# A fused transformer block: block 0's last attention sums travel by GpSimd's queue, and GpSimd starts splitting weights sooner

## The chip, the cores and the metric

The kernel runs on one core of one Trainium2 chip. The metric is device time in microseconds (us). Before the change the median of 3 runs was 1417.01 us (1413.06 to 1418.36).

## The reference

2048 rows of 512 features pass an attention layer with 32 query heads of 16 features that share one key and one value head, and then a gated feed-forward layer of width 1792. All is float32.

```python
h  = x + A(layernorm(x))          # A: q = x@wq (32 heads), k = x@wk, v = x@wv (one head)
                                  #    p = softmax(q k^T / 4); o = p v; A = o @ wo
h2 = h + B(layernorm(h))          # B: (gelu(x@w_gate) * (x@w_up)) @ w_down
```

## The kernel before

**Tiling.** The rows are cut into 4 blocks of 512 queries (`NB`), the heads into 8 groups of 4 (`NG`), the keys into 16 chunks of 128 (`KC`). For each block, group and chunk there are two `score` calls (L1031), numbered by `n`. One call makes 2 x 2 score matmuls `s<-qg,kaug` (L414) and one exponential `p<-s` on ScalarE (L418). After the second call of a chunk, four matmuls `acc<-p,v_sb` (L422) add the weighted values, some calls later (`finish`, L1008). A group takes 32 calls, block 0 takes 256. The query tile `qg` of a group is loaded from the DRAM buffer `q_d` one group ahead.

**The end of a group.** `evacuate` (L433) copies the finished PSUM sums to `oT` on VectorE (L435). They have to change partitions: SyncE stores `oT` to the DRAM buffer `acc_d` (L439), and `turn_out` (L444) reads it back in four transfers of 64 KB into `oc` (L448). For every second group VectorE then takes the reciprocal of the softmax sums in four pieces (L462), multiplies (L465), and splits the result into a high and a low part, `o_hi` (L473) and `o_lo` (L477). Four such columns c = 0 to 3 make up a block. For block 0 the store and the read of all groups but the last are spread over later calls. For its last group, `g == 7`, both are written straight behind the copy.

**The dense part.** A block's dense part begins with the output projection `pp<-wo,o` (L613, called from `project`, L660). It needs all four columns of `o_hi` and `o_lo`, in the order c = 0 to 3, and the split weights `wo`, which SyncE loads in two transfers of 1 MB (L587). For block 0, `load_wo(0)` stands in the program at `n == 256` (L1093), behind the last use of the pool "early", whose memory its tiles take over. The first `pp` matmul stands 16 calls later. Further on SyncE loads rows of x for the residual (`xb`, L647) and the first four gate and up weights (`w<-w_d`, L573, 512 KB each).

**Splitting the weights.** While block 0's attention runs, GpSimd prepares 46 pieces of weight (`part_weights`, L514): 4 of `wo`, and 14 each of gate, up and down. A raw piece of 256 KB is loaded on SyncE's queue (`load_f`, L520, issued at L522), two pieces ahead, into one of four buffers. GpSimd copies its high part and subtracts for its low part (L121, L122, called from `part_f`, L525), and stores both, 512 KB, one part later from one of two buffers (L531 and L537). The loop over `n` calls `next(parts)` at fixed counts (L1120): before the change at 16, 26 and 30 in the first group of 32, then seven times in each group.

**Bounds.** For each block of queries a bound `m` on the scores is worked out on GpSimd (L273 to L290) and stored to `q_d` (L294), two loop steps after its input is ready (`age`, L325). The tile of block 3's bound is in the pool "early", so `load_wo(0)` waits for this store too.

**What sets the order.** The engines run their own instruction streams, each in the written order. PE, ScalarE and GpSimd are scheduled by hand throughout, SyncE and VectorE in the loop over `n`. SyncE issues its transfers to one queue, GpSimd to another. An instruction waits for semaphores, and whatever stands behind it on its engine waits with it.

Of the kernel before, what the change touches and what calls it, by code (L numbers as in the profile page):

```python
# [32 lines left out]
AHEAD_W = 2  # L33
# [7 lines left out]
HURRY = ((0, 3), (1, 0), (1, 1))  # L41

START = 8

MIXED = {0: ("mms", 2), 3: ("smm", 1), 6: ("mm", 1), 8: ("ss", 1)}

# [8 lines left out]
def kernel(  # L55
# [12 lines left out]
    nc = tc.nc  # L68
# [3 lines left out]
    DH = wk.shape[1]  # L72
# [8 lines left out]
    NG = H // 4  # L81
    KC = S // P
# [28 lines left out]
    acc_d = dram.tile([P, 4, T], F32, name="acc_d")  # L111
# [5 lines left out]
    def split(eng_hi, hi, lo, src, eng_lo=None):  # L117
        if eng_hi is nc.scalar:
            nc.scalar.activation(hi, src, AF.Copy)
        else:  # L120
            eng_hi.tensor_copy(hi, src)  # L121
        (eng_lo or nc.vector).tensor_tensor(lo, src, hi.bitcast(F32), op=ALU.subtract)  # L122
# [29 lines left out]
    def attend(first):  # L152
        with ExitStack() as outer:
            with tc.manual_schedule(
                engines={mybir.EngineType.PE, mybir.EngineType.Pool, mybir.EngineType.Activation}
            ):
                run(outer, first)


    def run(outer, first):  # L160
# [164 lines left out]
        def age():  # L325
            for entry in after:
                entry[0] -= 1
            while after and after[0][0] <= 0:
                after.pop(0)[1]()
# [99 lines left out]
        def take_out():  # L429
            for step in outs.pop(0):  # L430
                step()

        def evacuate(b, g, acc):  # L433
            oT = sb.tile([P, T], F32, tag="oT", bufs=2, name=f"oT_{b}_{g}")
            nc.vector.tensor_copy(oT, acc)  # L435
            c, k = divmod(g, 2)
            last = b == NB - 1 and g == NG - 1
            if not last:
                nc.sync.dma_start(acc_d[:, g % 4, :], oT)  # L439
            if k == 0:  # L440
                pair[0] = sb.tile([P, 2, T], F32, tag="oc", bufs=2, name=f"oc_{b}_{c}")
            oc = pair[0]

            def turn_out():  # L444
                view = acc_d[:, g % 4, :].rearrange("(j s e) t -> j e s t", s=2, e=DH)
                for j in range(4):
                    r0 = 64 * k + DH * j
                    nc.sync.dma_start(oc[r0 : r0 + DH, :, :], view[j])  # L448

            def gather():  # L450

                for s in (1, 0):
                    for j in range(4):
                        r0 = 64 * k + DH * j
                        (nc.sync if s or j == 0 else nc.scalar).dma_start(
                            oc[r0 : r0 + DH, s, :], oT[(2 * j + s) * DH : (2 * j + s + 1) * DH, :]
                        )


            def invert(t):  # L460
                sl = slice(t * P, (t + 1) * P)
                nc.vector.reciprocal(oc[:, 1, sl], oc[:, 1, sl])  # L462

            def divide():
                nc.vector.tensor_tensor(oc[:, 0, :], oc[:, 0, :], oc[:, 1, :], op=ALU.mult)  # L465

            def high():
                if c == 0:
                    o_blk[b] = [
                        sb.tile([P, DC, T], F32R, tag=f"o_{w}", bufs=1, name=f"o_{w}_{b}")  # L470
                        for w in ("hi", "lo")
                    ]
                nc.vector.tensor_copy(o_blk[b][0][:, c, :], oc[:, 0, :])  # L473

            def low():
                hi, lo = o_blk[b]
                nc.vector.tensor_tensor(  # L477
                    lo[:, c, :], oc[:, 0, :], hi[:, c, :].bitcast(F32), op=ALU.subtract
                )


            def piece(t):
                sl = slice(t * P, (t + 1) * P)
                hi, lo = o_blk[b]
                invert(t)
                nc.vector.tensor_tensor(
                    oc[:, 0, sl], oc[:, 0, sl], oc[:, 1, sl], op=ALU.mult
                )
                split(nc.vector, hi[:, c, sl], lo[:, c, sl], oc[:, 0, sl], nc.gpsimd)

            if b == 0 and g < NG - 1:
                outs.append([turn_out])
            elif not last:
                turn_out()
            if last:
                last_out.extend([piece, gather])
            elif k == 1:

                if b == 0:
                    outs.extend([[] for _ in range(11)])  # L500
                    outs.extend([partial(invert, t)] for t in range(TB))
                    outs.extend([step] for step in (divide, high, low))
                else:
                    outs.append([])
                    outs.extend([partial(invert, t), partial(invert, t + 1)] for t in (0, 2))
                    outs.append([divide, high, low])
            if b == 0 and g == NG - 1:
                while outs:
                    take_out()
# [4 lines left out]
        def part_weights(pw):  # L514

            def load_f(src, name):  # L520
                raw = pw.tile([P, D], F32, tag="w_raw", bufs=AHEAD_W + 2, name=f"{name}r")
                nc.sync.dma_start(raw.rearrange("p (c n) -> p c n", n=src.shape[-1]), src)  # L522
                return raw

            def part_f(name, raw):  # L525
                both = pw.tile([P, 2, D], F32R, tag="w_both", bufs=2, name=f"{name}b")
                split(nc.gpsimd, both[:, 0], both[:, 1], raw, nc.gpsimd)
                return both

            def store_1(f, k, both):  # L530
                nc.gpsimd.dma_start(  # L531
                    w1_d[2 * f + k].bitcast(F32),
                    both.rearrange("p i (c n) -> p i c n", c=DC).bitcast(F32),
                )

            def store_2(dst, both):
                nc.gpsimd.dma_start(dst.bitcast(F32), both.bitcast(F32))  # L537

            steps = [
                (  # L540
                    partial(load_f, wo_t[:, c : c + 1, :], f"wo{c}"),
                    partial(part_f, f"wo{c}"), partial(store_2, wo_d[c]),
                )
                for c in range(DC)
            ]
            for f in range(FC):
                fs = slice(f * P, (f + 1) * P)
                for k, src in enumerate((wg_t, wu_t)):
                    name = f"w1{f}_{k}"
                    steps.append((  # L550
                        partial(load_f, src[:, :, fs], name),
                        partial(part_f, name), partial(store_1, f, k),
                    ))
                name = f"w2{f}"
                steps.append((
                    partial(load_f, wd_t[:, f : f + 1, :], name),
                    partial(part_f, name), partial(store_2, w2_d[f]),
                ))
            raws, left = {i: steps[i][0]() for i in range(AHEAD_W)}, None
            for i, (_, part, store) in enumerate(steps):  # L560
                if left is not None:
                    left()
                if i + AHEAD_W < len(steps):
                    raws[i + AHEAD_W] = steps[i + AHEAD_W][0]()
                both = part(raws.pop(i))
                left = partial(store, both)
                yield 1
            left()
# [491 lines left out]
        n, lead = 0, 2 * PER + sum(SIZES[: LEAD[0]])  # L1060
        with tc.manual_schedule(engines={mybir.EngineType.SP, mybir.EngineType.DVE}):
            parts = None
            if first:
                work = later_q()
                parts = part_weights(early.enter_context(tc.tile_pool(name="parts", bufs=1)))

            token, left = None, 6 * (NB - 1) * DC * DC
            while n < lead:
                age()
                r = n % (2 * KC) if n >= 2 * KC else n - START if n < 28 else 30  # L1070
                if first and n == START:
                    token = next(work)
                if (token is None or token == REST and left <= 0) and (n < START or n % 2 == 0):
                    kinds, runs = "ss", 1
# [7 lines left out]
                if n == 2 * PER:  # L1082
# [7 lines left out]
                    parts = work = None  # L1090
# [25 lines left out]
                for _ in range(runs):  # L1116
                    if outs and not pause[0] and n % (2 * KC) not in (2, 3, 4):
                        take_out()
                    pause[0] = max(pause[0] - 1, 0)
                if parts is not None and n > 12 and n % (2 * KC) % 10 in (0, 6):  # L1120
                    next(parts, None)
            assert n == lead
        assert not outs
# [21 lines left out]
        for c in range(LEAD[0], (NB - 1) * NG * len(SIZES)):  # L1145
            b, cb = divmod(c, NG * len(SIZES))
# [400 lines left out]
```

## Time and profile before

| | us |
|---|---|
| median of 3 runs | 1417.01 |
| lowest, highest | 1413.06, 1418.36 |
| the profiled execution, own time | 1414.98 |
| its span, first to last instruction | 1413.2 |
| its mean granted TensorE clock | 0.997 |

The profiled execution lies 2.03 us below the median, and 1.78 us of its time are outside the span. All times of events below count from the start of the span. In the rows of a timeline the columns are start, duration, engine, line, operation, output<-input with the form, count, and in brackets the idle time ahead of it with what ended it. "SPq" rows are SyncE's issues of transfers: the time is that of issuing, not of moving. In the chain of waits a row is start, length and what the chain passes through. In the table of windows each engine's busy time stands with its instructions in brackets, then PEclk, the granted TensorE clock as a share of full speed, the busy share of the DMA engines, and GB/s.

### The profile page before, as it was taken

Reading aid. Unit: us, or ns where it says so; the run is one execution under the profiler, and the core shown is the slowest. Engines: PE = TensorE matmul, PEld = TensorE weight load, DVE = VectorE, ACT = ScalarE, POOL = GpSimd, SP = SyncE. Lnnn points to the kernel's source line nnn. Section 1 sums busy time; section 2 is a strip of 40 time slices with the busy share of each in tenths; the row PEclk is TensorE's granted clock in tenths of the full one; section 3 lists DMA queues with packets and bytes.
Section 4 is the critical chain, followed back from the end, with each engine's and each line's share of the span. In section 5 each row is a group of like instructions: output and inputs, shape, how many; then the busy total and the mean of one; then the engine's idle time right before and its main releaser. Section 6 shows DMA issues by size and latency. Waiting matters only on the chain.

```text
span 1413.2 us, 25646 instructions
## 1 busy us (share of the span) xinstructions
PE 1393.7 (99%) x10646; PEld 784.9 (56%) x10646; DVE 548.3 (39%) x982; ACT 1041.6 (74%) x1149; POOL 188.7 (13%) x286
## 2 busy tenths in 40 slices
PE   8999999999999999999999999999999999999998
PEld 7433333334555555555555555554565555557886
DVE  7322322324252433424252432513353342427665
ACT  7799999996777777777787777877788777772000
POOL 6455655521000000000000000000000000002000
PEclk9999999999999999999999999999999999999999
DMA  4477787762342332223252332223243241335551
GB/s 159 148 222 250 247 252 248 227 216 90 102 157 64 117 117 87 87 84 142 83 176 72 116 117 87 87 90 118 102 139 108 87 146 50 137 122 198 186 196 60
DMA packets 84969, 194.11 MB, mean 137 GB/s; under 512 B 9904, under 2 KB 24240, under 8 KB 84812
## 3 DMA queue, kind: packets, MB, share of 16 engines
q1 hardware_dynamic: 77572, 167.50, 35.4%
q0 software_dynamic: 7104, 24.78, 4.8%
q8 instruction: 86, 1.41, 0.4%
q14 instruction: 39, 0.32, 0.1%
q10 hardware_dynamic: 168, 0.10, 0.0%
HBM read 142.52 MB, written 49.55 MB: 136 GB/s over the span
## 4 chain that ended last, share of the span: by engine, by line
PE 92%; ACT 3%; DMA 2%; DVE 1%; issue 1%; POOL 0%; SPq 0%; DVEq 0%; ACTq 0%; POOLq 0%
PE acc L422 33%; PE s L414 18%; PE pu L936 9%; PE pg L936 8%; PE pd L936 4%; PE pq L412 4%; PE pd L613 3%; ACT p L418 3%; PE pd L635 3%; PE pg L635 3%; PE pu L635 3%; PE pp L613 2%; PE pp L744 1%; DMA acc_d<-oT 1%; PE pxt L680 1%
## 5 line engine op out<-in xcount | busy, mean ns | idle before, releaser
L418 ACT ACTIVATE p<-s 128x1024 f32<-128x1024 f32 x1024 | 970.2, 1032 | 229.0 <-PE s L414 226.0
L422 PE MATMUL acc<-p,v_sb 128*32 128x512 f32 x4096 | 496.9, 600 | 0.0
L414 PE MATMUL s<-qg,kaug 50*128 50x512 f32 x1984 | 418.1, 425 | 3.5 <-ACT p L418 3.5
L414 PEld LDWEIGHTS s<-qg,kaug 50*128 50x128 f32 x1984 | 195.1, 185 | 218.5 <-ACT p L418 121.5
L422 PEld LDWEIGHTS acc<-p,v_sb 128*32 128x32 f32 x4096 | 109.8, 109 | 229.0 <-issue 225.5
L936 PE MATMUL pu<-x2h,w 64*128 64x512 f32 x672 | 212.1, 391 | 0.0
L936 PE MATMUL pg<-x2h,w 64*128 64x512 f32 x672 | 211.7, 391 | 0.0
L936 PEld LDWEIGHTS pu<-x2h,w 64*128 64x128 f32 x672 | 116.0, 186 | 14.5
L936 PEld LDWEIGHTS pg<-x2h,w 64*128 64x128 f32 x672 | 116.3, 186 | 13.1 <-DVE h L878 0.5
L936 PE MATMUL pg<-x2l,w 64*128 64x512 f32 x336 | 122.3, 391 | 0.0
L936 PE MATMUL pu<-x2l,w 64*128 64x512 f32 x336 | 121.9, 390 | 0.0
L813 ACT ACTIVATE ga<-ga 128x512 f32<-128x512 f32 x56 | 35.3, 634 | 89.2 <-DVE ga L808 89.2
L131 POOL TENSOR_SCALAR rstd<-mv 128x1 f32<-128x1 f32 x16 | 3.5, 220 | 682.9 <-DVE mv L129 682.8
L936 PE MATMUL pd<-w,gh 64*128 64x512 f32 x384 | 81.2, 392 | 0.0
L878 DVE TENSOR_TENSOR h<-h,pd 128x512 f32<-128x512 f32 x48 | 31.9, 685 | 115.4 <-PE pd L936 66.4
L462 DVE RECIPROCAL oc<-oc 128x128 f32<-128x128 f32 x64 | 56.6, 923 | 32.4 <-DMA oc<-acc_d 27.6
L1172 DVE SCALAR_TENSOR_TENSOR ga<-ga,g 128x512 f32<-128x512 f32 x70 | 48.3, 691 | 52.3 <-ACT ga L813 51.3
L797 DVE COPY g<-pg 128x512 f32<-128x512 f32 x56 | 38.7, 692 | 63.0 <-PE pg L936 57.3
L936 PEld LDWEIGHTS pu<-x2l,w 64*128 64x128 f32 x336 | 58.0, 186 | 6.8
L936 PEld LDWEIGHTS pg<-x2l,w 64*128 64x128 f32 x336 | 58.2, 186 | 6.4
L435 DVE COPY oT<-acc 128x512 f32<-128x512 f32 x32 | 22.1, 692 | 96.8 <-PE acc L422 96.6
L810 DVE SCALAR_TENSOR_TENSOR g<-g,pu 128x512 f32<-128x512 f32 x56 | 38.2, 683 | 40.4 <-PE pu L936 30.5
(246 smaller groups left out, 1458.0 us busy)
## 6 DMA issues: line engine op xcount, KB each, us to landing
w<-w_d SPq DMA_DIRECT2D x112, 512.0 KB
w<-w_d SPq DMA_DIRECT2D x28, 1024.0 KB
qg<-q_d SPq DMA_DIRECT2D x48, 200.0 KB
q_d<-qh SPq DMA_DIRECT2D x32, 256.0 KB
wo<-wo_d SPq DMA_DIRECT2D x8, 1024.0 KB
acc_d<-oT SPq DMA_DIRECT2D x31, 256.0 KB
oc<-acc_d SPq DMA_DIRECT2D x124, 64.0 KB
w_d<-w_0b POOLq DMA_DIRECT2D x14, 512.0 KB, 7.3
```

The lines of the kernel that those rows point to most:

```text
L412: step()
L414: nc.tensor.matmul(s[:, a, :], kaug[rows, kc * P : (kc + 1) * P], qg[rows, 2 * u + a, :], start=True, stop=True,)
L418: nc.scalar.activation(p[:, 2 * u : 2 * u + 2, :], s, AF.Exp, scale=SCALE)
L422: nc.tensor.matmul(acc[32 * j : 32 * j + 32, :], v_sb[:, kc, :], p[:, j, :], start=(kc == 0), stop=(kc == KC - 1), skip_group_check=True,)
L462: nc.vector.reciprocal(oc[:, 1, sl], oc[:, 1, sl])
L613: nc.tensor.matmul(banks[k], lhsT[rows], rhs[rows], start=(turn == 0 and i == 0), stop=(turn == 1 and i == n - 1), skip_group_check=True,)
L635: nc.tensor.matmul(bank, lhsT, rhs, start=(i == 0), stop=(i == len(ts) - 1))
L797: nc.vector.tensor_copy(g, pg)
L810: nc.vector.scalar_tensor_tensor(g, g, 0.5, pu, op0=ALU.mult, op1=ALU.mult)
L813: nc.scalar.activation(a, a, AF.Tanh, scale=GELU_A * GELU_C)
L936: nc.tensor.matmul(e["bank"], lhsT[rows], rhs[rows], start=i == 0 and not e["both"], stop=last and e["both"], skip_group_check=True,)
L1172: (soon or lazy).pop(0)()
```

## The change

It has three parts.

1. For block 0's last group alone, the store of `oT` to `acc_d` and the four reads into `oc` are issued by GpSimd and no longer by SyncE.
2. The first two raw pieces, of `wo`, are loaded by GpSimd and no longer by SyncE.
3. `next(parts)` is called at n = 8, 11, 16, 21, 26 and 30 in the first group (it was 16, 26 and 30). All later parts stand three calls of `next` earlier.

```diff
+EARLY_PARTS = (8, 11, 16, 21, 26)
...
             last = b == NB - 1 and g == NG - 1
+            queue = nc.gpsimd if b == 0 and g == NG - 1 else nc.sync
             if not last:
-                nc.sync.dma_start(acc_d[:, g % 4, :], oT)
+                queue.dma_start(acc_d[:, g % 4, :], oT)
...
-                    nc.sync.dma_start(oc[r0 : r0 + DH, :, :], view[j])
+                    queue.dma_start(oc[r0 : r0 + DH, :, :], view[j])
...
-            def load_f(src, name):
+            def load_f(src, name, queue=nc.sync):
                 raw = pw.tile([P, D], F32, tag="w_raw", bufs=AHEAD_W + 2, name=f"{name}r")
-                nc.sync.dma_start(raw.rearrange("p (c n) -> p c n", n=src.shape[-1]), src)
+                queue.dma_start(raw.rearrange("p (c n) -> p c n", n=src.shape[-1]), src)
...
-            raws, left = {i: steps[i][0]() for i in range(AHEAD_W)}, None
+            raws, left = {i: steps[i][0](queue=nc.gpsimd) for i in range(AHEAD_W)}, None
...
-                if parts is not None and n > 12 and n % (2 * KC) % 10 in (0, 6):
+                if parts is not None and (
+                    n in EARLY_PARTS or n > 2 * KC - 4 and n % (2 * KC) % 10 in (0, 6)
+                ):
                     next(parts, None)
```

Line numbers after the change are higher by 2 to 5.

The first place is the end of block 0 on SyncE. Its stream before, from the bound check `b_d` to block 0's first dense weights; `qg` and `xb` belong to block 1's second group and block 0's dense part:

```order
L1469 DMA b_d<-q2m 32x1
L587 DMA wo_0_3388<-wo_d 128x2x1024
L587 DMA wo_1_3390<-wo_d 128x2x1024
L439 DMA acc_d<-oT_7_3419 128x512
L448 DMA oc_3_3128<-acc_d 16x2x512 x4
L394 DMA qg_1_3433<-q_d 50x2x512 x2
L647 DMA xb_0_3458<-in_A_x_dram 128x512
L647 DMA xb_1_3460<-in_A_x_dram 128x512
```

The same stretch of SyncE's stream after the change:

```order
L1474 DMA b_d<-q2m 32x1
L590 DMA wo_0_3388<-wo_d 128x2x1024
L590 DMA wo_1_3390<-wo_d 128x2x1024
L396 DMA qg_1_3433<-q_d 50x2x512 x2
L650 DMA xb_0_3458<-in_A_x_dram 128x512
L650 DMA xb_1_3460<-in_A_x_dram 128x512
```

The store and the four reads have left it, and `qg`, `xb` and what follows no longer stand behind them. On GpSimd at that place, before, behind the last weight piece `w213` and block 3's bound `m`, the dense part's `rstd` came next:

```order
L537 DMA w_d<-w213b 128x1024
L273 TENSOR_SCALAR mm_0_3298<-q_70,k2m 32x1
L276 TENSOR_TENSOR mm_0_3298<-mm_0_3298,power 32x1
L279 TENSOR_SCALAR mm_0_3298<-mm_0_3298 32x1
L282 TENSOR_SCALAR mm_0_3298<-mm_0_3298,k2m 32x1
L290 TENSOR_SCALAR m_0_3299<-qn_0_3295,mm_0_3298 32x512
L294 DMA q_d<-m_0_3299 32x512
L131 TENSOR_SCALAR rstd_0_0_3662<-mv_0_0_3659 128x1
```

After the change:

```order
L540 DMA w_d<-w213b 128x1024
L275 TENSOR_SCALAR mm_0_3298<-q_70,k2m 32x1
L278 TENSOR_TENSOR mm_0_3298<-mm_0_3298,power 32x1
L281 TENSOR_SCALAR mm_0_3298<-mm_0_3298 32x1
L284 TENSOR_SCALAR mm_0_3298<-mm_0_3298,k2m 32x1
L292 TENSOR_SCALAR m_0_3299<-qn_0_3295,mm_0_3298 32x512
L296 DMA q_d<-m_0_3299 32x512
L442 DMA acc_d<-oT_7_3419 128x512
L451 DMA oc_3_3129<-acc_d 16x2x512 x4
L133 TENSOR_SCALAR rstd_0_0_3662<-mv_0_0_3659 128x1
```

The five transfers stand between the bound and `rstd`. The second place is the start of the weight pieces on GpSimd; `kaug` is the last work for the keys. Before:

```order
L1359 TENSOR_TENSOR kaug<-vT_685,kaug 16x512 x2
L1359 TENSOR_TENSOR kaug<-vT_688,kaug 16x512 x2
L121 CAST wo0b<-wo0r 128x512
L122 TENSOR_TENSOR wo0b<-wo0r,wo0b 128x512
L537 DMA wo_d<-wo0b 128x1024
```

After:

```order
L1364 TENSOR_TENSOR kaug<-vT_685,kaug 16x512 x2
L1364 TENSOR_TENSOR kaug<-vT_688,kaug 16x512 x2
L525 DMA wo0r<-in_A_wo_dram 128x512
L525 DMA wo1r<-in_A_wo_dram 128x512
L123 CAST wo0b<-wo0r 128x512
L124 TENSOR_TENSOR wo0b<-wo0r,wo0b 128x512
L540 DMA wo_d<-wo0b 128x1024
```

GpSimd issues the first two raw loads itself, ahead of the first split. The streams of PE, ScalarE and VectorE hold the same instructions in the same order before and after.

## The prediction

> **What bounds the kernel now.** I read the page first: its busy times and the chain of work that ended last.
>
> ```profile
> PE 1393.7 (99%) x10646; PEld 784.9 (56%) x10646; DVE 548.3 (39%) x982; ACT 1041.6 (74%) x1149; POOL 188.7 (13%) x286
> PE 92%; ACT 3%; DMA 2%; DVE 1%; issue 1%; POOL 0%; SPq 0%; DVEq 0%; ACTq 0%; POOLq 0%
> ```
>
> PE is the bound nearly everywhere, so the change can earn only where PE stands still. The 2% of DMA in the chain deserve a look. In the chain in order of time they lie at the end of block 0:
>
> ```profile
> 299.21 1.17 ACT p L418
> ...
> 300.42 0.38 SPq L587
> 300.85 0.46 SPq L587
> ...
> 301.37 8.47 DMA acc_d<-oT
> ...
> 311.16 2.17 DMA oc<-acc_d
> ...
> 313.52 3.40 DVE oc L462 x4
> 316.95 0.70 DVE oc L465
> 317.67 0.44 DVE o_hi L473
> ...
> 318.16 1.02 PE pp L613 x4
> ```
>
> The store of 256 KB needs 8.47 us. Ahead of it on SyncE's queue stand the two `wo` loads (L587, 2 MB). The table of windows shows what the DMA engines did, and the timeline of PE what the wait costs:
>
> ```profile
> 298.00:300.00 2.00, 2.00 (x16) 0.53 (x12) 0.00 (x0) 2.00 (x3) 0.00 (x0) 1.00 0.00 0
> 302.00:304.00 2.00, 2.00 (x14) 0.60 (x14) 0.00 (x0) 2.00 (x4) 0.00 (x0) 1.00 0.92 365
> 318.29:321.70 3.41, 3.41 (x18) 1.56 (x22) 0.69 (x2) 1.94 (x2) 0.00 (x0) 0.52 1.03 414
> 311.42 0.49 PE L414 MATMUL s<-qg,kaug 50*128 50x512 f32 x2 [0.34 <-ACT p L418]
> 313.19 0.73 PE L613 MATMUL pp<-wo,o_hi 64*128 64x512 f32 x4 [0.34 <-DMA oc<-acc_d]
> 315.59 0.42 PE L414 MATMUL s<-qg,kaug 50*128 50x512 f32 x2
> 318.16 1.02 PE L613 MATMUL pp<-wo,o_hi 64*128 64x512 f32 x4 [2.14 <-DVE o_hi L473]
> ```
>
> At 365 GB/s the 2 MB alone last 5.7 us. PE starts `pp` at 313.19 with columns c = 0 to 2, and stands still for 2.14 us until 318.16, when column 3 of `o_hi` is there. Then comes a second loss: from 318.29 to 321.70 the granted clock is 0.52, with PE busy throughout, which costs (1 - 0.52) x 3.41 = 1.64 us. So the stall is worth at most 2.14 + 1.64 = 3.8 us, with the short wait at 313.19 4.1 us. Until 312 ScalarE's exponentials set PE's pace (its short waits are for `p`), and after 324 PE has work again, so a shorter stall moves all that follows.
>
> The Trainium skill, "TensorE: Matmul & The Clock Gate" (Part 1), says that the clock falls to half after a window of about 3.4 us with too little work, and that these windows run freely, not tied to the kernel. The row's 0.52 over 3.41 us agrees; by the page the 1.64 us would be paid in some executions only, and the sum would lie between -1.9 and -3.5.
>
> **The change, part by part.**
>
> *The store and the four reads on GpSimd.* What GpSimd's queue takes, and when the inputs are ready:
>
> ```profile
> 295.54 0.59 POOL L294 DMA_DIRECT2D q_d<-m  x1 [0.29 <-DMA oc<-acc_d]
> 331.07 0.24 POOL L131 TENSOR_SCALAR rstd<-mv 128x1 f32<-128x1 f32 x1 [34.94 <-DVE mv L129]
> 300.14 0.69 DVE L435 COPY oT<-acc 128x512 f32<-128x512 f32 x1 [11.34 <-PE acc L422]
> 49.77 1.04 POOL L348 DMA_DIRECT2D qg_first<-q_d  x2
> wo_d<-wo0b POOLq DMA_DIRECT2D x1, 512.0 KB, 2.9
> w_d<-w_0b POOLq DMA_DIRECT2D x14, 512.0 KB, 7.3
> w_d<-w211b POOLq DMA_DIRECT2D x1, 512.0 KB, 8.7
> q_d<-m POOLq DMA_DIRECT2D x3, 64.0 KB, 4.6
> qg_first<-m POOLq DMA_DIRECT2D x4, 2.0 KB, 6.5
> ```
>
> GpSimd is idle from 296.13 to 331.07, so the five issues, 0.59 + 4 x 0.52 = 2.7 us (two issues took 1.04), fall into idle time; behind them stands only `rstd`, wanted at 331. `oT` is ready at 300.83. A store of 256 KB on this queue was not measured. Bounds: 2.9 us from issue to landing, for 512 KB with little beside it, and 8.7 us, for 512 KB beside SyncE's transfers. I take 4.5: at half the bytes, half of what the crowd adds (7.3 - 2.9 = 4.4), on a base of a little under 2.9. It lands at 305.3 (303.7 to 309.5). The reads of 64 KB: the nearest row is 4.6 us for 64 KB, the bounds 2.9 and 6.5. The fourth is issued 3 x 0.52 = 1.56 us later, so `oc` is complete at 305.3 + 1.56 + 4.6 = 311.5 (308.2 to 317.6). Now it is complete at 311.16 + 2.17 = 313.33. That is 1.9 us earlier, by the bounds 5.1 us earlier to 4.3 us later.
>
> The stall ends with `o_hi`, 4.8 us behind `oc` by the chain: at 316.3, while PE is through with the matmuls ahead at 316.01. A wait of 0.2 us remains, and PE is then short of 0.2 us of work, not of 2.14, so I count the half clock as gone: -1.9 - 1.6 = **-3.5 us**. What is late next is nothing I can see: the following `pp` and `acc` matmuls have their data.
>
> What SyncE issues next gets freed by this:
>
> ```profile
> 311.63 0.75 SPq L394 DMA_DIRECT2D qg<-q_d  x2
> 312.43 0.83 SPq L647 DMA_DIRECT2D xb<-in_A_x_dram  x2
> 313.30 2.27 SPq L573 DMA_DIRECT2D w<-w_d  x4
> ```
>
> These 2.9 MB (0.4, 0.5 and 2) now start at about 301, beside the store. This is the crowd that I charged above. For `wo` itself the company costs the store's and reads' 0.5 MB at 365 GB/s, 1.4 us: from about 309.8, when the store behind it landed, to 311.2, still ahead of the first `pp` at 313.19. Without that cover each us would be one of PE.
>
> The Trainium skill, "DMA: Bandwidth & Descriptors" (Issuing engines are not separate DMA queues), speaks against this part: transfers from SyncE and GpSimd run on the same 16 engines and interleave, and a second issuer saves only issue time. By it the sum would be about -0.5; it is the first rival below. The same page (Queues, rings and completion order) has each engine take turns between queues packet by packet, which would let a small store pass 2 MB; the rows of 512 KB landing in 7.3 us beside a busy SyncE queue agree.
>
> *The first two raw loads on GpSimd, and earlier parts.*
>
> ```profile
> 52.83 5.29 POOL L1359 TENSOR_TENSOR kaug<-vT,kaug 16x512 fp32r<-16x512 f32 x4
> 63.96 0.46 SPq L522 DMA_DIRECT2D wo0r<-in_A_wo_dram  x1
> 73.01 0.61 POOL L121 CAST wo0b<-wo0r 128x512 fp32r<-128x512 f32 x1 [14.90 <-PE s L414]
> qg_first<-q_d POOLq DMA_DIRECT2D x2, 192.0 KB, 4.3
> 287.77 0.67 DVE L268 TENSOR_REDUCE q<-qn 32x1 f32<-32x512 f32 x1
> 292.77 0.26 POOL L273 TENSOR_SCALAR mm<-q,k2m 32x1 f32<-32x1 f32 x1
> ```
>
> GpSimd waits 14.90 us for its first piece, which SyncE asks for only at 63.96. Asked for at 58.1 by GpSimd, it lands some 4.3 us later (192 KB row), and splitting starts near 62.5, 10.5 us sooner. The third piece still comes by SyncE, so the lead may shrink to 5 us. GpSimd's last piece and the bound behind it end sooner: its input is ready at 288.4, and it starts at 292.77, so up to 4.3 us are in it. The store of the bound releases the `wo` loads, now at 300.42. Starting at 296.1 they find the DMA engines empty (298 to 300). But PE does not wait for `wo`, so this counts **0**; it thins the crowd around the store.
>
> What is late instead: in GpSimd's stream the bounds move behind up to three more parts, and SyncE's raw loads stand one to three places further ahead of other transfers.
>
> ```profile
> SPq L522 <- POOL w_1b L122: 30.0, 8, 6.5
> 91.08 0.72 SPq L394 DMA_DIRECT2D qg<-q_d  x2
> L435 DVE COPY oT<-acc x2: 692/692/693, 86.2 to 116.6; 128x512 f32<-128x512 f32 x2
> ```
>
> SyncE waits for GpSimd to free a raw buffer, 6.5 us at most, and a query tile may stand behind it. The tile loaded at 91.08 is first read when group 1's sums are done, near 116: 25 us of cover. If this were gone, PE would wait us for us. I take 0, and +3 as the upper bound.
>
> Sum: 1414.98 - 3.5 = 1411.5 against the profiled execution. That lies 2.0 us under the median of the runs, so against the median the forecast is 1417.0 - 3.5 = **1413.5 us**.
>
> **The rivals.**
>
> 1. *The queue makes no difference.* The DMA engines serve `wo`, and the newly freed loads, ahead of or along with the store; it lands near 309, and `oc` at 313 as now. For it: 365 GB/s with 2 MB queued, and now 2.9 MB more. Against it: 512 KB stores that pass a busy queue in 7.3 us. Time: -0.5 to 0, **1416.5 to 1417**.
> 2. *Slower: GpSimd's two trips take longer than SyncE's.* Two landings follow each other there, 8.7 and 1.56 + 6.5 us by the upper rows: `oc` at 317.6, 4.3 us later than now. The stall grows to 6.4 us, and a second half-clock stretch adds up to 1.7. It decides from 313.33 on: whatever of `oc` lands later is lost. Time: +4.3 to +6, **1421.3 to 1423**. For it: four reads of one small size, each with the whole fixed latency. Against it: the upper rows were measured with several transfers queued on GpSimd's own queue, which is empty at 300.8.
> 3. *All of the stall goes and the short wait at 313.19 too*: -4.1, **1412.9**.
>
> **How the numbers follow.** The forecast, with rival 3 as its end, has a chance of 0.7, rival 1 of 0.15, rival 2 of 0.1, and 0.05 is left for a wait in the first 290 us. The forecast's own range is 1413 to 1415.5; the runs of before spread from 1413.06 to 1418.36, so I add 2.5 us below, and above I go to 1418.5, which takes in rival 1. About 0.5%, 7 us, is what a measurement of this kernel can tell from no change. The forecast and rivals 1 and 3 lie within it, and most of rival 2: same 0.88, slower 0.08, faster 0.04.
>
> **What would show it.** In the profile of after: the store's landing 4 to 5 us behind its issue, `oc` complete near 311.5, `pp`'s wait for `o_hi` under 0.5 us, no stretch of half clock around 318; the first split near 62.5 and the `wo` loads issued ahead of 300. The prediction is wrong if `oc` comes after 313, if PE waits for `wo` at its first `pp`, or if a query tile comes late before 300.

## The result, and the profile after

The changed kernel takes **1421.23 us**, the median of 8 runs (1418.84 to 1421.89), against 1416.34 us for 8 runs of the kernel before: a ratio of **1.0035, 95% interval 1.0023 to 1.0047**. It is slower, by about 5 us of 1416, with the whole interval above 1, where I had forecast 1413.5 us and no more than 1418.5. Its profiled execution took 1418.84 us, with a span of 1417.1 against 1413.2.

The loss is where the gain was expected. The chain of waits after, at the end of block 0 (start, length, what it passes through):

```profile
301.11 7.08 DMA acc_d<-oT
308.47 1.04 POOL oc L451 x2
...
310.17 6.55 DMA oc<-acc_d
...
316.75 3.40 DVE oc L465 x4
...
321.37 1.22 PE pp L616 x3
```

The store leaves 0.3 us earlier than before, 301.11 against 301.37, and takes 7.08 us. The reads take from 308.47 to 316.72, 8.25 us from the first issue to the last landing; SyncE's took 3.5 us (309.85 to 313.33). `oc` comes 3.4 us later than before. PE pays for that, in its timeline, and the table of windows shows its clock behind it (the last three columns are granted clock, DMA share and GB/s):

```profile
321.37 1.22 PE L616 MATMUL pp<-wo,o_hi 64*128 64x512 f32 x4 [5.36 <-DVE o_hi L476]
```

```profile
302.00:304.00 2.00, 2.00 (x14) 0.57 (x14) 0.00 (x0) 2.00 (x4) 0.00 (x0) 1.00 1.03 379
308.00:310.00 2.00, 2.00 (x17) 0.55 (x15) 0.00 (x0) 2.00 (x3) 1.37 (x3) 1.00 1.03 352
312.00:314.00 2.00, 1.32 (x10) 1.00 (x12) 0.00 (x0) 2.00 (x3) 0.00 (x0) 1.00 1.02 266
320.00:322.00 2.00, 0.63 (x4) 0.53 (x6) 1.90 (x4) 0.00 (x0) 0.00 (x0) 0.50 0.00 0
322.00:324.00 2.00, 2.00 (x14) 1.15 (x14) 0.20 (x2) 0.88 (x1) 0.00 (x0) 0.50 0.00 0
```

The stall is 5.36 us instead of 2.14. The half clock lasts longer too, but PE stood still through much of it, so its price is about the old one. The DMA share is 1.0 from 302 to 314; before, it was 0.16 to 0.53 in the windows from 308 to 314, while the reads ran. One of these windows of before:

```profile
310.00:312.00 2.00, 1.57 (x12) 0.34 (x10) 0.00 (x0) 2.00 (x3) 0.00 (x0) 1.00 0.28 87
```

SyncE's timeline after says why:

```profile
297.60 0.90 SPq L590 DMA_DIRECT2D wo<-wo_d  x2
298.55 1.13 SPq L396 DMA_DIRECT2D qg<-q_d  x2
299.72 0.84 SPq L650 DMA_DIRECT2D xb<-in_A_x_dram  x2
300.60 5.43 SPq L576 DMA_DIRECT2D w<-w_d  x4
```

SyncE no longer waits for the store. It asks for `qg`, `xb` and `w` (2.9 MB) 13 us earlier, all of it by 306, just ahead of GpSimd's reads. The trace's DMA packets, counted by queue (packets, MB, share of the 16 engines), show what the reads then meet. From the first read's issue at 308.47 to 312.25 only SyncE's queue, `q1`, moves anything:

```profile
q1 hardware_dynamic: 467, 1.48, 102.4%
```

So four reads stand issued for up to 3.8 us before the first of their bytes moves.

To compare runs at this place I use the stretch from the `oT` copy of block 0's last group to the next group's copy, since what PE loses here lies in it and executions differ by up to 2.8 us ahead of it. VectorE's timeline, before (the first copy, at 300.14, stands in the prediction) and then after:

```profile
339.07 0.69 DVE L435 COPY oT<-acc 128x512 f32<-128x512 f32 x1 [1.32 <-PE acc L422]
```

```profile
300.12 0.69 DVE L437 COPY oT<-acc 128x512 f32<-128x512 f32 x1 [11.34 <-PE acc L424]
342.25 0.69 DVE L437 COPY oT<-acc 128x512 f32<-128x512 f32 x1 [1.32 <-PE acc L424]
```

The **stretch** is 38.93 us before and 42.13 after, 3.2 us more, as the stall. Up to 300 us the two profiles agree (300.14 and 300.12). The last 0.7 us of the span's 3.9 come later, mostly from a wait of 0.75 us for a weight near 718, which comes back below.

### The profile page after: what moved, and what is told of

Same layout as the page of the kernel before. It is cut to its first block, busy times and chain, and to the rows that moved or that the text cites. A ratio compares the mean times of both kernels' runs of the same rounds, so it can differ in the third digit from the quotient of the medians.

```text
span 1417.1 us, 25653 instructions
## 1 busy us (share of the span) xinstructions
PE 1394.7 (98%) x10646; PEld 783.2 (55%) x10646; DVE 549.4 (39%) x982; ACT 1041.1 (73%) x1149; POOL 194.1 (14%) x293
## 4 chain that ended last, share of the span: by engine, by line
PE 92%; ACT 3%; DMA 2%; DVE 1%; issue 1%; POOL 0%; SPq 0%; DVEq 0%; ACTq 0%; POOLq 0%
PE acc L424 33%; PE s L416 18%; PE pu L939 9%; PE pg L939 7%; PE pd L939 4%; PE pq L414 4%; PE pd L616 3%; PE pd L638 3%; PE pg L638 3%; PE pu L638 3%; ACT p L420 2%; PE pp L616 2%; PE pp L747 1%; DMA acc_d<-oT 1%; DMA oc<-acc_d 1%
```

## The experiments

**Theory A**: the trip of `oT` through DRAM is as long as what stands in the DMA engines' way, whichever engine issues it, and the change put 2.9 MB there. **Theory B**: GpSimd's queue is slow for this trip by itself. **Theory C**: the earlier weight parts cost the time. Ten more runs followed; a ratio is always to runs of the kernel before made alongside. What nine of them and the two first profiles showed of the trip, one execution each, with "lead" for how long ahead of the store the `wo` loads were issued, and "trip" from the start of the `oT` copy to VectorE's first operation on `oc`:

| kernel | store / reads by | lead | store | reads | trip | stretch |
|---|---|---|---|---|---|---|
| before | SyncE / SyncE | 0.95 | 8.47 | 3.5 | 13.4 | 38.93 |
| before, again (e8) | SyncE / SyncE | 0.95 | 8.51 | 3.6 | 13.6 | 37.71 |
| after | GpSimd / GpSimd | 3.51 | 7.08 | 8.25 | 16.6 | 42.13 |
| e1, part 1 alone | GpSimd / GpSimd | 2.02 | 8.28 | 8.3 | 18.1 | 45.14 |
| e2, parts 2 and 3 | SyncE / SyncE | 3.72 | 6.12 | 3.5 | 10.4 | 35.54 |
| e3, 64-row hold | GpSimd / GpSimd | 3.72 | 6.88 | 4.0 | 12.2 | 42.50 |
| e4, reads by SyncE | GpSimd / SyncE | 5.16 | 4.40 | 3.6 | 9.0 | 35.48 |
| e10, e4 again | GpSimd / SyncE | 4.10 | 5.67 | 3.6 | 10.3 | 35.55 |
| e5, `wo` behind | SyncE / SyncE | none | 3.57 | 3.5 | 7.8 | 40.25 |
| e6, loads held | GpSimd / GpSimd | 5.01 | 4.33 | 4.1 | 9.8 | 35.51 |
| e7, `wo` held too | GpSimd / GpSimd | none | 3.19 | 4.1 | 8.5 | 42.70 |

Two sums of this table carry the argument. Where `pp` waits for `o_hi` and VectorE was not held up otherwise (before, e8, after, e1), the trip less the stall is 11.2 to 11.3 us each time; trips of 7.8 to 10.4 us cause no wait for `o_hi`. So every us of trip beyond some 11.25 is one of stall. And in all nine rows with a lead, lead and store add up to 9.3 to 10.6 us: the store lands about that long behind the issue of `wo`, whoever issues it.

**e1: part 1 alone.** The kernel before, with the store and the reads on GpSimd and nothing else.

```diff
+            queue = nc.gpsimd if b == 0 and g == NG - 1 else nc.sync
...
-                nc.sync.dma_start(acc_d[:, g % 4, :], oT)
+                queue.dma_start(acc_d[:, g % 4, :], oT)
...
-                    nc.sync.dma_start(oc[r0 : r0 + DH, :, :], view[j])
+                    queue.dma_start(oc[r0 : r0 + DH, :, :], view[j])
```

> Part 1 alone: block 0's last store and its four reads are issued by GpSimd, while all raw loads stay with SyncE and the parts keep their old places. Theory A (the freed SyncE loads crowd the round trip): wo is asked for at 300.4 again, 2.8 us later than in the changed kernel, and the 2.9 MB of qg, xb and w1 follow without a wait, so store and reads share the DMA engines with 4.9 MB: oc complete at 316.7 to 319.5, ratio to before 1.003 to 1.006. Theory B (GpSimd's trip is slow by itself): the same landings as in the changed kernel, oc at 316 to 317, ratio 1.003 to 1.004. Theory C (the early parts and raw loads are what costs): oc near 313, ratio 1.000 or below.

Measured: 1421.94 us, ratio 1.0035 (1.0018 to 1.0052). GpSimd's and PE's timelines:

```profile
302.32 0.59 POOL L440 DMA_DIRECT2D acc_d<-oT  x1 [6.76 <-DVE oT L435]
310.87 2.04 POOL L449 DMA_DIRECT2D oc<-acc_d  x4 [7.97 <-DMA acc_d<-oT]
```

```profile
324.06 1.22 PE L614 MATMUL pp<-wo,o_hi 64*128 64x512 f32 x4 [6.84 <-DVE o_hi L474]
```

Part 1 alone has the loss, with a stall of 6.84 us and `oc` at 319.2, where theory A had it: theory C falls, and theory B's 316 to 317 is missed too. `wo` is asked for at 300.30 here, so the store meets more of it than in the changed kernel.

**e2: parts 2 and 3 alone.** The changed kernel with SyncE's store and reads back.

```diff
-            queue = nc.gpsimd if b == 0 and g == NG - 1 else nc.sync
+            queue = nc.sync
```

> Parts 2 and 3 alone: the raw loads by GpSimd and the early parts stay, store and reads go back to SyncE. Theories A and B agree: wo is asked for at 297.6, so its 2 MB are moved some 2.8 us earlier than in the kernel before, the store behind them on SyncE lands at 304 to 306.5 instead of 309.85, the reads take the 3.5 us that they took in the kernel before, oc is complete at 308 to 310, pp waits under 0.3 us and the half-clock stretch near 318 is gone: ratio to before 0.9970 to 0.9985. Theory C: the ratio is that of the changed kernel, 1.002 to 1.004, without a late oc.

Measured: 1414.99 us, ratio 0.9993 (0.9974 to 1.0012). SyncE's timeline, and VectorE's:

```profile
299.04 0.90 SPq L590 DMA_DIRECT2D wo<-wo_d  x2
302.76 0.34 SPq L442 DMA_DIRECT2D acc_d<-oT  x1
308.89 1.73 SPq L451 DMA_DIRECT2D oc<-acc_d  x4
```

```profile
302.04 0.69 DVE L437 COPY oT<-acc 128x512 f32<-128x512 f32 x1 [11.33 <-PE acc L424]
312.43 3.39 DVE L465 RECIPROCAL oc<-oc 128x128 f32<-128x128 f32 x4 [9.70 <-DMA oc<-acc_d]
337.58 0.69 DVE L437 COPY oT<-acc 128x512 f32<-128x512 f32 x1 [1.32 <-PE acc L424]
```

The parts that I had counted at 0 take the whole stall away: `wo` is 3 us ahead of `oT`, the trip is 10.4 us (I expected `oc` 8 to 10 us behind the copy; the excess is in the store, 6.12 us), and the stretch is 35.54 us, 3.4 less than in the first profile of before. Column 3 of `o_hi` is there in time:

```profile
317.74 0.67 PE L616 MATMUL pp<-wo,o_hi 64*128 64x512 f32 x4
```

Of the time as a whole the runs show no difference; its interval still holds the 0.9976 that 3.4 us would give.

**e3: the freed loads held by a store of 64 rows.** The changed kernel, with a wait for `oc` put on SyncE.

```diff
                     queue.dma_start(oc[r0 : r0 + DH, :, :], view[j])
+                if b == 0 and g == NG - 1:
+                    nc.sync.dma_start(hold_d, oc[64 * k : 64 * k + 64, 0, :1])
```

> The changed kernel with one more transfer on SyncE, a 256-byte store of a column of oc to a scratch tensor in DRAM, behind the wo loads: it waits for the four reads, and so holds back qg, xb and w1 until oc has landed, as the reads themselves did in the kernel before. Theory A: the store meets only what is left of wo and lands at 304 to 306, the reads find idle DMA engines and are done by 308.5 to 311, pp waits under 0.3 us, no half-clock stretch at 318, ratio to before 0.9970 to 0.9985. Theory B: store at 307 to 308.5, reads 6 us more, oc at 315 to 317, ratio 1.003 or more.

Measured: 1420.41 us, ratio 1.0027 (1.0009 to 1.0045). The ratio says nothing on the theories, because the hold had a price of its own, in the chain of waits:

```profile
303.06 6.88 DMA acc_d<-oT
...
311.92 2.34 DMA oc<-acc_d
...
314.28 7.90 DMA hold_d<-oc
```

VectorE's multiply writes the column that the 256 bytes are read from, and they needed 7.90 us. But the reads were through in 4.0 us (310.22 to 314.26), as theory A had it. The store is another matter: it landed at 309.94, and theory A had 304 to 306. It met no freed load, only `wo`, asked for 3.72 us ahead of it, and of the delay 1.9 us are the execution's own, whose `oT` copy starts at 302.06.

**e4: the store on GpSimd, the reads on SyncE.**

```diff
-                    queue.dma_start(oc[r0 : r0 + DH, :, :], view[j])
+                    nc.sync.dma_start(oc[r0 : r0 + DH, :, :], view[j])
```

> The changed kernel with the four reads of block 0's last sums back on SyncE and only the store on GpSimd: SyncE waits for the store's landing, so qg, xb and w1 come behind the reads. Theory A: the store meets only what is left of wo and lands at 304 to 306, the reads take 3.5 us as on SyncE before, oc at 308 to 310, ratio to before 0.9970 to 0.9985. Theory B (a GpSimd transfer takes 7 us whatever runs beside it): store at 307 to 308.5, oc at 311 to 312, pp waits up to 0.5 us, ratio 0.9975 to 0.999.

Measured: 1415.08 us, ratio 0.9989 (0.9971 to 1.0008). GpSimd's store and SyncE's loads and reads:

```profile
302.46 0.59 POOL L442 DMA_DIRECT2D acc_d<-oT  x1 [9.23 <-DVE oT L437]
```

```profile
297.30 0.90 SPq L590 DMA_DIRECT2D wo<-wo_d  x2
306.87 1.74 SPq L451 DMA_DIRECT2D oc<-acc_d  x4
308.71 0.69 SPq L396 DMA_DIRECT2D qg<-q_d  x2
```

The store lands 4.40 us behind its issue. That is close to the 4.5 of my prediction, but by luck: it goes with a lead of 5.16 us that I had not worked out. The waiting SyncE keeps the freed loads off the reads. The stall and the half clock are gone in this profile. **e10** is the same kernel once more:

> The run with the store on GpSimd and the reads on SyncE once more, for its ratio (0.9989 with an interval that reaches over 1) and for a second profile: from oT of block 0's last group to oT of the next one 35.5 us again, 3.45 less than in the kernel before, and at 712 us a wait of pu for w1 between 0 and 2.5 us, as it varies from execution to execution. Ratio 0.9975 to 0.9995.

Measured: 1416.1 us, ratio 0.999 (0.9973 to 1.0007), a stretch of 35.55 us, and no wait near 712. Both times the estimate is below 1 and the interval reaches over it. A gain over the kernel before is not shown. That this version is faster than the changed kernel is: both intervals end below 1.0023, where the changed kernel's begins.

**e5: `wo` behind the trip.** The kernel before, with the `wo` loads written later.

```diff
-                    load_wo(0)
...
                 if n == 2 * PER + 8:
+                    load_wo(0)
                     primed = dense(0)
```

> The kernel before with one edit: the two wo loads are written after block 0's last store, its reads and the qg load, so SyncE issues them behind, not ahead. No transfer is on GpSimd. Theory A (what stands in the round trip's way decides, not the engine that issues it): with nothing large ahead the store lands 2.1 us after its issue (as the unhindered store of the kernel before at 705.89, whose reads were issued at 707.96), the reads take the 3.5 us of before, oc is complete 6.5 us behind oT against 12.5 us in the kernel before; pp's wait on o_hi and the half-clock stretch at 318 go, 3.5 us less from oT to the first s row behind pp. wo then starts some 5 to 6 us later and lands near 313; a wait of pp for wo of up to 1.5 us would give part of it back. Ratio 0.997 to 0.9995. Rival (the wo load bounds pp): the stall stays, now on wo, ratio 1.000 to 1.002.

Measured: 1417.51 us, ratio 1.0017 (0.9997 to 1.0037). SyncE's and PE's timelines:

```profile
301.01 0.34 SPq L439 DMA_DIRECT2D acc_d<-oT  x1
304.58 1.71 SPq L448 DMA_DIRECT2D oc<-acc_d  x4
307.47 0.91 SPq L587 DMA_DIRECT2D wo<-wo_d  x2
```

```profile
315.93 1.22 PE L613 MATMUL pp<-wo,o_hi 64*128 64x512 f32 x4 [2.95 <-DMA xb<-in_A_x_dram]
```

The store falls from 8.47 to 3.57 us with no GpSimd in it, so theory A holds for the store in the kernel before too. My 2.1 us were too short, and so was the 1.5 us for `wo`: the first `pp` waits 2.95 us. The profile names `xb`, the transfer that came last; `pp` reads `wo`, asked for 0.96 us ahead of it. The rival won here, and the clock went with it: 0.58 and 0.57 in the windows 314 to 318 and 318 to 322.

**e6: the freed loads held cleanly.** The changed kernel, with the hold on a copy that nobody else needs.

```diff
                     queue.dma_start(oc[r0 : r0 + DH, :, :], view[j])
+                if b == 0 and g == NG - 1:
+                    held = sb.tile([P, 1], F32, tag="held", bufs=1, name="held")
+                    nc.vector.tensor_copy(held[64:], oc[64:, 0, :1])
+                    nc.sync.dma_start(hold_d, held[64:65])
```

> The changed kernel, with SyncE held between the wo loads and qg, xb and w1 until oc has landed: VectorE copies a column of oc (64x1) to a small tile behind the four reads, and a 4-byte store of that tile is put on SyncE. VectorE's own work waits for the copy alone, not for the store, unlike in the run with the 64-row hold. Theory A: the store still meets wo (4.4 us where wo was asked for 4 to 5 us ahead of it, up to 7 where both come together), the reads take 4 us from first issue to the last landing instead of 8.25, oc is complete 9.5 to 12.5 us behind oT (16.6 in the changed kernel), pp waits 0 to 2 us; ratio 0.9975 to 1.000. Theory B (GpSimd's trip is slow by itself): reads 8 us, oc 16 us behind oT, ratio 1.003.

Measured: 1415.46 us, ratio 1.0004 (0.9986 to 1.0022). GpSimd's timeline, and VectorE's:

```profile
302.46 0.59 POOL L443 DMA_DIRECT2D acc_d<-oT  x1 [9.23 <-DVE oT L438]
307.07 1.04 POOL L452 DMA_DIRECT2D oc<-acc_d  x2 [4.02 <-DMA acc_d<-oT]
308.28 1.00 POOL L452 DMA_DIRECT2D oc<-acc_d  x2 [0.17 <-issue]
```

```profile
311.22 0.15 DVE L455 COPY held<-oc 64x1 f32<-64x1 f32 x1 [9.06 <-DMA oc<-acc_d]
336.97 0.69 DVE L438 COPY oT<-acc 128x512 f32<-128x512 f32 x1 [1.33 <-PE acc L425]
```

This is the run that decides. Store and reads are on GpSimd as in the changed kernel, and the edit only makes the freed loads later. The reads take 4.1 us instead of 8.25, and while they run, from 307.07 to 310.6, nothing is seen of SyncE's queue, and the reads move on GpSimd's, `q0`:

```profile
q0 software_dynamic: 128, 0.26, 32.2%
```

The stretch is 35.51 us instead of 42.13. Not all of that is the edit's: in this execution `wo` has 1.5 us more lead, and the store takes 4.33 us instead of 7.08. Theory B, which had 8 us for the reads, falls, and the interval of the ratio ends at 1.0022, just below that of the changed kernel. The estimate itself lies a little above my range.

**e7: `wo` held as well.** The same, and `load_wo(0)` moved as in e5.

> The same, with the wo loads behind the hold as well: GpSimd's store and reads run with no large load beside them. A measurement, not a candidate: wo is asked for only when oc has landed, so pp will wait for wo. Theory A: store 2.5 to 3.5 us from issue to landing, reads 4 us from first issue to last landing, oc complete 7.5 to 9 us behind oT, 1 to 2.5 us more than SyncE's own uncrowded trip in the run with wo behind. Theory B: store 7 us, oc 15 us or more behind oT.

Measured, one run: 1421.3 us. In GpSimd's timeline the store, issued at 302.61, has landed before the reads start:

```profile
306.08 1.05 POOL L452 DMA_DIRECT2D oc<-acc_d  x2 [2.88 <-DMA acc_d<-oT]
```

The store takes 3.19 us and the reads 4.1. GpSimd's own trip is then 8.5 us against SyncE's 7.8 in e5: in these two executions the queue costs 0.7 us. PE waits 5.63 us for `wo`, as meant.

**e8: the kernel before, again**, unchanged.

> The kernel before once more, for a second profile of it: at the end of block 1 (712 us), where the runs with a shorter round trip lost 2.3 us to a w1 load that took 6.2 us, the first profile shows no wait. If that wait is the price of having gained time at block 0's end, it is absent here too; if it comes and goes with each execution, it may show here, 0 to 2.5 us. The stall of pp at block 0's end is 2.1 us again and the half-clock stretch is there.

Measured, one run: 1417.65 us. PE's timeline in two places, and the table of windows:

```profile
321.14 0.73 PE L613 MATMUL pp<-wo,o_hi 64*128 64x512 f32 x4 [2.36 <-DVE o_hi L473]
```

```profile
716.47 0.47 PE L936 MATMUL pu<-x2h,w 64*128 64x512 f32 x1 [1.01 <-DMA w<-w_d]
```

```profile
318.00:322.00 4.00, 1.64 (x16) 0.94 (x14) 3.71 (x6) 1.89 (x2) 0.00 (x0) 1.00 0.99 353
```

The stall is there, 2.36 us, but the clock stays at 1.00: the half clock that I had counted as part of every execution is in the first profile and not in this one. And a wait of 1.01 us for a weight near 716, absent from the first profile, is here.

**e9: later groups on GpSimd too.** e4, and from block 1 on the store and the reads of every group but the last on GpSimd.

```diff
-            queue = nc.gpsimd if b == 0 and g == NG - 1 else nc.sync
+            queue = nc.gpsimd if b > 0 or g == NG - 1 else nc.sync
...
-                    nc.sync.dma_start(oc[r0 : r0 + DH, :, :], view[j])
+                    (nc.gpsimd if b else nc.sync).dma_start(oc[r0 : r0 + DH, :, :], view[j])
```

> The run with the store on GpSimd and the reads on SyncE, and besides, from block 1 on, the store and the reads of every group but the last on GpSimd, which is nearly idle there: SyncE never waits for a store to land, so the w1 load at the end of block 1, issued behind the four reads (707.48, 1.81 us behind the first of them, in the run without this edit), goes out at least 2 to 4 us earlier and the wait of pu for it at 712 us (2.24 us there, 1.01 in the second profile of before) goes. From theory A the GpSimd trips of the later groups take 8 to 15 us beside the weight loads instead of 4 to 6, which has some 10 us of slack only if the group's reciprocals are not due at once: if that slack is there, ratio 0.996 to 0.999; if a pp of a later block waits for a late oc, ratio 1.000 to 1.005.

Measured: 1454.04 us, ratio 1.0246 (1.0214 to 1.0277). From VectorE's timeline, and from PE's:

```profile
390.41 1.76 DVE L465 RECIPROCAL oc<-oc 128x128 f32<-128x128 f32 x2 [7.04 <-DMA oc<-acc_d]
```

```profile
392.77 0.79 PE L939 MATMUL pg<-x2h,w 64*128 64x512 f32 x1 [3.32 <-DVE g L813]
```

The second case of the expectation came, five times dearer than I gave it. The reciprocals stand at a fixed place in VectorE's stream; when `oc` is late, VectorE waits, and with it the operations that PE's next matmuls wait for, as `pg` here. Over the kernel VectorE waits 65.4 us for `oc`, 27.6 before, and `pg` waits 21.2 us in four places for VectorE's copy `mark_pg`. The wait of `pu` for `w1` is gone, as expected.

## Why the prediction was wrong, point by point

**The bound and the place: right.** Most of what the change moved, 3.2 of the 3.9 us of span, lies in the stall before `pp` at the end of block 0. In the stretch, a trip that ends early enough is worth what I had forecast: with stall and half clock gone it is 3.4 us shorter in e2, e4, e6 and e10 than in the first profile, against my -3.5. In the time as a whole none of them shows it.

**The store, 4.5 us: mis-sized, 7.08.** I halved a crowd, and named the freed 2.9 MB as that crowd. The runs show that the store's time follows the lead of `wo`, the 2 MB that I had let thin out: 8.5 us with 0.95 us of lead, 8.3 with 2.0, 6.1 to 7.1 with 3.5 to 3.7, 5.7 with 4.1, 4.4 with 5.1, and 3.2 to 3.6 with none in the way, on either queue. The freed loads add little to it: e3, without them, needs 6.88 at nearly the lead of the changed kernel. The issuer matters little, but not nothing: at a lead of 3.72 us SyncE's store took 6.12 (e2) and GpSimd's 6.88 (e3). My 4.5 fits a lead of 5 us.

**The reads, 1.56 + 4.6 us: mis-sized, 8.25.** This is the failed step in the sentence "This is the crowd that I charged above". The crowd was charged to the store and not to the reads, for which I took the row of 64 KB at 4.6 us. Without the crowd they need 4.1 us (e6, e7), even less than I took; with it twice that. The wait of SyncE that the change removes had kept the DMA engines free for the reads. That was its use, and I had priced only its cost. Against the kernel before the store became 1.4 us shorter and the reads 4.7 us longer, so it is the reads that turned a gain into a loss.

`oc` came at 316.7, not at 311.5, 5.2 us late: 2.6 in the store, 2.1 in the reads, and 0.28 us twice from a ready input to GpSimd's issue, which I had put at nothing. **Rival 2**, "GpSimd's two trips take longer than SyncE's", is what came, at the lower end of its price: `oc` at 317.6 there, 316.7 here; 1421.3 to 1423 us there, 1421.23 here. Its reason was wrong, though: not "four reads of one small size, each with the whole fixed latency", since e7 has them done in 4.1 us, but the freed loads. That its price fits is partly luck: the stall is 5.36 us, not its 6.4, and part of the 4.9 us stays unexplained below. I gave it 0.1 because the slow rows had been "measured with several transfers queued on GpSimd's own queue". What made those rows slow was not tried; the store and the reads here were slow on an empty queue of their own, beside SyncE's traffic.

**The half clock, -1.6: half right.** It goes with the stall, but e8 shows that the kernel before doesn't pay it each time. The Trainium skill, "TensorE: Matmul & The Clock Gate" (Part 1), has the windows run freely; 0.52 in the first profile of before and 1.00 in the second, behind stalls of 2.14 and 2.36 us, agree. The stretch of e8 is 37.71 us, so a trip without a stall is worth 2.2 to 3.4 us, not always 3.5.

**Parts 2 and 3, counted 0: wrong.** The steps were right: the first split stands at 63.39 (62.5 forecast), the `wo` loads go out at 297.60, ahead of 300, and no query tile came late. In the timeline of GpSimd after:

```profile
63.39 0.61 POOL L123 CAST wo0b<-wo0r 128x512 fp32r<-128x512 f32 x1 [4.05 <-DMA wo0r<-in_A_wo_dram]
```

But "PE does not wait for `wo`, so this counts 0" missed that the store does wait for it. An earlier `wo` alone clears the store's way and takes the stall of the kernel before (e2). What I had as a side effect was the useful part, and what I had as the gain undid it.

**The rule against the change: right.** The Trainium skill, "DMA: Bandwidth & Descriptors" (Issuing engines are not separate DMA queues), says that transfers started by different engines share the same 16 engines, so that a second issuer saves issue time alone. I made it a rival of 0.15 and then took a second queue as a way past 2 MB. Trips of 8.5 us by GpSimd and 7.8 by SyncE with nothing large beside them, and stores of 8.28 and 8.47 with `wo` 2 and 1 us ahead, agree with it. The turns between the queues, from which the prediction had a small store pass 2 MB, do not show: in the changed kernel GpSimd's queue moved nothing for 4.1 us behind the issue of its store and 3.8 us behind that of its reads, while SyncE's moved 1.5 MB each time; with nothing large beside it, in e7, the first byte of its store came 1.2 us after the issue.

**What stays open.** The changed kernel's median lies 4.9 us above that of before; the stretch explains 3.2 against the first profile and 4.4 against the second, one execution each. The rest, and why e2 and e6 show no shorter time as a whole, may have to do with a wait of `pu` for a `w1` load at the end of block 1:

```profile
713.83 0.47 PE L939 MATMUL pu<-x2h,w 64*128 64x512 f32 x1 [2.24 <-DMA w<-w_d]
```

That row is e4's. The same wait is 2.33 us in e2, 2.22 in e6, 1.52 in e1, 1.01 in e8, 0.75 in the changed kernel, and absent in the first profile of before, in e3, e5, e7 and e9 and in e10, which is e4 unchanged. So it comes and goes with the execution and isn't a price of the shorter trip alone. What decides it was not found. Nor does a run tell whether reads issued by a third engine would have been as slow beside the freed loads as GpSimd's, or why GpSimd's bytes start so late there.

## What to carry to other kernels

A wait on a queue does two things: it delays what stands behind it, and it keeps that traffic away from whatever the wait is for. Before you move a waiting transfer to another queue, list what the old queue will issue in the same microseconds, and charge it to every leg of the trip, the last one above all. A large load that no engine waits for still has a price if a small urgent transfer runs behind it, so look at what it stands in the way of before you count its move at nothing.

## What the runs showed that I had not expected

- The time of a 256 KB store follows how long ahead a 2 MB load was issued, far more than the issuing engine: 8.5 us at 1 us of lead, 4.4 at 5, 3.2 to 3.6 with nothing there.
- A store of 64 rows of 4 bytes took 7.90 us to land (e3), more than the 256 KB store in the same run, 6.88. SyncE's 2.9 MB were issued right behind it.
- Two profiles of one kernel differ by 2.76 us at the `oT` copy of block 0's last group (300.14 and 302.90), as they do at its first one, 86 us. The half clock around 55 us lasts some 3.4 us in the first and 10.2 in the second, by the windows of 2 us there; at half price the 6.8 us between them are worth at most 3.4, but that they are the cause was not tried.
